# Three small tiles are allocated ahead of the large ones, which shifts the place of the large ones in a partition

## The chip, the cores and the metric

One core of one Trainium2 chip runs the whole kernel. The metric is the device time of one execution in microseconds. TensorE appears in the profile as PE (matmuls) and PEld (weight loads), VectorE as DVE, ScalarE as ACT, GpSimd as POOL, and the queue that issues most DMAs as SP.

## The reference

Two attention blocks with 32 inducing rows (m = 32) over 12480 rows of 128 channels, then two MLPs of width 2048:

```python
def mab(q, kv):
    s = scale * (q @ kv.transpose(0, 2, 1))
    s = s - s.max(-1, keepdims=True)
    a = np.exp(s)
    a /= a.sum(-1, keepdims=True) + 1e-09
    return a @ kv
h = mab(I, x)          # I: the inducing rows
y = mab(x, h)          # 12480 x 128
# first MLP
h1 = y @ w_in;  y2 = (h1 * np.cos(h1)) @ w_out
# second MLP
h2 = y2 @ w_in2; out = (h2 / (1 + np.exp(-h2))) @ w_out2
```

## The kernel before, in words

**Front.** The first part loads x, transposes it, computes the first attention with a running maximum, and folds the second attention's value product into the first MLP: `hw0` to `hw3` are the 32 rows of h times `w_in1`, four copies stacked in the 128 partitions. So the first MLP's input matmul takes the attention weights (`stk`) as its moving operand.

**Steps.** The rest is one long loop over steps, with the order written out by hand. The rows are cut into 25 blocks of up to 512 columns: 22 of 512, then 480, 448 and 288. Each block takes 8 steps (NJ = 8), and a step handles 256 of the 2048 hidden rows in two halves. In a full step TensorE does 20 matmuls, each with a 128x128 weight load of its own, in this order:

1. `mlp1_in` (line 761): 2 matmuls, weights `hw`, moving `stk`.
2. `mlp2_in` (line 896): 6 matmuls for the block that is L2 = 11 steps behind. The operands are split in a high and a low part, three products for each half: weights `wi2_0`, `wi2_1`, `wi2_0`, moving `yhi`, `yhi`, `ylo`.
3. `mlp2_out` (`down`, line 843): 6 matmuls, weights `wo2_0` and `wo2_1`, moving `hi2` and `lo2`, two steps further behind.
4. `mlp1_out` (`down` again, line 843): 6 matmuls, weights `wo1_0` and `wo1_1`, moving `hi1` and `lo1`.

Steps 3 and 4 are the same function on other tiles, so in the profile both stand at line 843 as `acc<-hi,wo` and `acc<-lo,wo` (buffer numbers are left out). They follow each other within a step, `wo2` first. In a few steps after a softmax exponential (`held_back`) `mlp2_in` comes later, and the order is 1, 3, 2, 4 or 1, 3, 4, 2.

The first 12 steps of the first MLP and the first 8 of the second use float32 weights (`wf1`, and `wf2` in `held`) with four matmuls of line 853 in the profile in place of the six of line 843. So of the steps whose block has 512 columns, 22 x 8 = 176, all have a `hw` group, 176 have a `wi2` group, 168 a `wo2` group and 164 a `wo1` group in three products.

Between the groups, ACT takes the cosine (line 796) and the SiLU (line 911) out of PSUM and makes the second MLP's high part (line 919), DVE makes the first MLP's product, high part and low part (lines 800, 807, 833), and POOL makes the second MLP's low part (line 920).

**Tiles.** The pool `persist` places its tiles one after the other in each partition, each rounded up to 32 bytes; the pools of the front (`pp`, `pw`) and of the steps (`u1`, `u2`, `blk`, `late`) lie behind it. The order in which the tiles are made thus sets their addresses.

Of the kernel before, what the change touches and what calls it, by code (L numbers as in the profile page):

```python
# [9 lines left out]
F32 = mybir.dt.float32  # L10
F32R = mybir.dt.float32r
BF16 = mybir.dt.bfloat16
I32 = mybir.dt.int32
# [9 lines left out]
def tile_induced_attention_then_two_mlps(  # L23
# [36 lines left out]
    P, G, Q = 128, 4, 32  # L60
# [6 lines left out]
    KT = 16  # L67
# [15 lines left out]
    persist = ctx.enter_context(tc.tile_pool(name="persist", bufs=1))  # L83

    half_pi = persist.tile([P, 1], F32, name="half_pi")
    quarter = persist.tile([P, 1], F32, name="quarter")
    s_w = persist.tile([P, 1], F32, name="s_w")
    hT4 = persist.tile([C, G, M], F32, name="hT4")

    held = persist.tile([P, G * W], F32, name="held")  # L90
# [3 lines left out]
    wf1 = persist.tile([P, NF, C], F32, name="wf1")  # L94
    hw = [persist.tile([P, FF // 4], F32R, name=f"hw{i}") for i in range(4)]
    wo1 = [persist.tile([P, NF, C], F32R, name=f"wo1_{i}") for i in range(2)]
    flag = persist.tile([1, 1], I32, name="flag")
    stk = persist.tile([P, 2, W], F32R, name="stk")

    sft = {  # L100
        "s2": persist.tile([P, KT, M], F32, name="s2"),
        "m2": persist.tile([P, KT, 1], F32, name="m2"),
        "sm": persist.tile([P, KT, 1], F32, name="sm"),
        "at": persist.tile([P, W], F32, name="at"),
        "hi": persist.tile([P, W], F32R, name="ahi"),
    }
# [1001 lines left out]
```

## Time and profile before

| | before |
|---|---|
| time, median of 3 runs | 967.84 us (967.08 to 967.96) |
| time of the profiled execution | 967.38 us |
| its span, first to last instruction | 965.2 us |
| PE busy | 951.8 us (99%) |
| DVE busy | 779.3 us (81%) |
| ACT busy | 691.6 us (72%) |
| POOL busy | 517.2 us (54%) |
[...]

A matmul's busy time in these views begins at its start and ends at a modelled end that reaches into the next matmul, so neighbouring ones overlap: how fast the engine advances is read from the distance between starts. A share of PE near 100% says that it has no visible gap, not that it runs at its peak.

### The profile page before, as it was taken

Reading aid. Unit: us, or ns where it says so; the run is one execution under the profiler, and the core shown is the slowest. Engines: PE = TensorE matmul, PEld = TensorE weight load, DVE = VectorE, ACT = ScalarE, POOL = GpSimd, SP = SyncE. Lnnn points to the kernel's source line nnn. Section 1 sums busy time; section 2 is a strip of 40 time slices with the busy share of each in tenths; the row PEclk is TensorE's granted clock in tenths of the full one; section 3 lists DMA queues with packets and bytes.
Section 4 is the critical chain, followed back from the end, with each engine's and each line's share of the span. In section 5 each row is a group of like instructions: output and inputs, shape, how many; then the busy total and the mean of one; then the engine's idle time right before and its main releaser. Section 6 shows DMA issues by size and latency. Waiting matters only on the chain.

```text
span 965.2 us, 11951 instructions
## 1 busy us (share of the span) xinstructions
PE 951.8 (99%) x4480; PEld 758.0 (79%) x4481; DVE 779.3 (81%) x784; ACT 691.6 (72%) x725; POOL 517.2 (54%) x274
## 2 busy tenths in 40 slices
PE   8899999999999999999999999999999999999997
PEld 5456778888878888878888887888887888888896
DVE  4889888988887988888988887988888888878751
ACT  5687768777668776767777777777767777677774
POOL 3346545654545655554655544655455554555565
PEclk9999999999999999999999999999999999999999
DMA  9341000001010010010010010010010100100001
GB/s 356 112 138 45 6 18 11 14 20 22 2 22 12 12 22 12 12 22 12 12 22 12 12 22 12 12 22 7 17 22 1 22 14 9 21 12 5 13 11 20
DMA packets 65484, 28.19 MB, mean 29 GB/s; under 512 B 54440, under 2 KB 60040, under 8 KB 65416
## 3 DMA queue, kind: packets, MB, share of 16 engines
q1 hardware_dynamic: 64760, 27.24, 10.8%
q8 instruction: 37, 0.61, 0.3%
q14 instruction: 31, 0.25, 0.1%
q10 hardware_dynamic: 656, 0.09, 0.1%
HBM read 14.79 MB, written 6.39 MB: 22 GB/s over the span
## 4 chain that ended last, share of the span: by engine, by line
PE 95%; DMA 2%; DVE 1%; issue 0%; SPq 0%; ACT 0%; POOL 0%; ACTq 0%; POOLq 0%; DVEq 0%
PE acc L843 53%; PE h L896 28%; PE h L761 9%; PE acc L853 4%; DMA x_sb<-in_x_dram 2%; PE s L211 1%; PE pt L392 0%; PE hp L539 0%; SPq L328 0%; PE s L419 0%; DVE et L507 0%; DVE c L800 0%; DVE mx L432 0%; POOL lo L925 0%; PE misc L455 0%
## 5 line engine op out<-in xcount | busy, mean ns | idle before, releaser
L920 POOL TENSOR_TENSOR lo<-s,hi 128x1024 fp32r<-128x1024 f32 (+3 forms) x189 | 446.7, 2364 | 381.0 <-ACT hi L919 359.6
L843 PE MATMUL acc<-hi,wo 128*128 128x512 f32 (+3 forms) x1520 | 406.8, 389 | 0.0
L843 PEld LDWEIGHTS acc<-hi,wo 128*128 128x128 f32 x1520 | 282.5, 188 | 61.5 <-issue 3.7
L800 DVE TENSOR_TENSOR h<-h,c 128x1024 f32<-128x1024 f32 (+3 forms) x188 | 226.1, 1203 | 123.9 <-ACT c L796 123.7
L796 ACT ACTIVATE c<-h,half_pi 128x1024 f32<-128x1024 f32 (+3 forms) x200 | 219.2, 1096 | 146.9 <-PE h L761 146.1
L911 ACT ACTIVATE s<-h 128x1024 f32<-128x1024 f32 (+3 forms) x200 | 201.2, 1006 | 76.6 <-PE h L896 71.8
L896 PE MATMUL h<-yhi,wi 128*128 128x512 f32 (+3 forms) x800 | 244.2, 386 | 0.0
L843 PE MATMUL acc<-lo,wo 128*128 128x512 f32 (+3 forms) x760 | 232.6, 387 | 0.1
L807 DVE CAST hi<-h 128x1024 fp32r<-128x1024 f32 (+3 forms) x188 | 224.9, 1196 | 6.5
L833 DVE TENSOR_TENSOR lo<-h,hi 128x1024 fp32r<-128x1024 f32 (+3 forms) x188 | 223.9, 1191 | 5.7
L919 ACT CAST hi<-s 128x1024 fp32r<-128x1024 f32 (+3 forms) x189 | 195.3, 1033 | 6.1
L896 PEld LDWEIGHTS h<-yhi,wi 128*128 128x128 f32 x800 | 148.8, 188 | 30.7 <-issue 0.5
L843 PEld LDWEIGHTS acc<-lo,wo 128*128 128x128 f32 x760 | 141.9, 188 | 31.2 <-POOL lo L925 0.4
L896 PE MATMUL h<-ylo,wi 128*128 128x512 f32 (+3 forms) x400 | 154.3, 386 | 0.0
L761 PE MATMUL h<-stk,hw 128*128 128x512 f32 (+3 forms) x400 | 126.0, 396 | 1.4 <-ACT stk L704 0.7
L761 PEld LDWEIGHTS h<-stk,hw 128*128 128x128 f32 x400 | 74.1, 188 | 26.8 <-issue 6.5
L896 PEld LDWEIGHTS h<-ylo,wi 128*128 128x128 f32 x400 | 75.1, 188 | 15.2
L877 ACT CAST yhi<-acc 128x512 fp32r<-128x512 f32 (+3 forms) x25 | 14.4, 576 | 15.1 <-PE acc L843 15.0
L943 DVE STREAM_TRANSPOSE o<-acc 128x512 f32<-128x512 f32 (+3 forms) x25 | 17.3, 694 | 9.3 <-PE acc L843 9.3
L853 PE MATMUL acc<-c,wf 128*128 128x512 f32 x48 | 22.5, 591 | 0.0
L878 DVE TENSOR_TENSOR ylo<-acc,yhi 128x512 fp32r<-128x512 f32 (+3 forms) x25 | 16.7, 669 | 5.4 <-ACT yhi L877 5.3
L800 DVE TENSOR_TENSOR c<-h,c 128x1024 f32<-128x1024 f32 x12 | 14.6, 1216 | 2.4 <-ACT c L796 1.9
(133 smaller groups left out, 320.6 us busy)
## 6 DMA issues: line engine op xcount, KB each, us to landing
out_dram<-o SPq DMA_DIRECT2D x80, 64.0 KB, 1.9
x_sb<-in_x_dram SPq DMA_DIRECT2D x8, 512.0 KB, 9.2
raw<-in_moe_w_in_dram SPq DMA_DIRECT2D x8, 512.0 KB, 6.5
raw<-in_moe_w_out_dram SPq DMA_DIRECT2D x8, 512.0 KB, 4.5
stk<-ahi SPq DMA_DIRECT2D x40, 64.0 KB, 2.0
stk<-at SPq DMA_DIRECT2D x40, 64.0 KB, 2.0
x_sb<-in_x_dram SPq DMA_DIRECT2D x3, 256.0 KB, 3.7
x_sb<-in_x_dram SPq DMA_DIRECT2D x2, 320.0 KB
```

Of the source, the lines that this page charges most:

```text
L761: nc.tensor.matmul(ps[:, a, 0:n], lhsT=hw[f // 4][:, f % 4 * P : (f % 4 + 1) * P], rhs=stacks[b][:, 0:n], start=True, stop=True,)
L796: nc.scalar.activation(cs, h, AF.Sin, bias=half_pi, scale=1.0)
L800: nc.vector.tensor_tensor(cs if whole else h, h, cs, ALU.mult)
L807: nc.vector.tensor_copy(hi[:, :, 0:n], h)
L833: nc.vector.tensor_tensor(lo[:, :, 0:n], h, hi[:, :, 0:n].bitcast(F32), ALU.subtract)
L843: nc.tensor.matmul(acc[:, 0:n], lhsT=wt[:, 2 * j + a, :], rhs=gt[:, a, 0:n], start=(j == 0 and p == 0 and a == 0), stop=(j == NJ - 1 and p ...
L853: nc.tensor.matmul(acc[:, 0:n], lhsT=w[:, 2 * j + a, :], rhs=c[:, a, 0:n], start=(j == 0 and a == 0), stop=(j == NJ - 1 and a == 1),)
L896: nc.tensor.matmul(ps[:, a, 0:n], lhsT=wt[:, fs], rhs=yt[:, 0:n], start=(p == 0), stop=(p == 2),)
L911: nc.scalar.activation(sv, hid2.pop(u)[:, :, 0:n], AF.Silu)
L919: nc.scalar.copy(hv, sv)
L920: nc.gpsimd.tensor_tensor(lv, sv, hv.bitcast(F32), ALU.subtract)
L943: nc.vector.transpose(o.rearrange("p t d -> p (t d)")[:, 0:n], acc2.pop(b)[:, 0:n])
```

## The change

`flag` (4 bytes in one partition), `m2` and `sm` (64 bytes each) are allocated right behind `s_w`, instead of behind `wo1` and `s2`. They take 32 + 64 + 64 = 160 bytes there. Nothing else is edited.

```diff
     s_w = persist.tile([P, 1], F32, name="s_w")
+    flag = persist.tile([1, 1], I32, name="flag")
+    m2 = persist.tile([P, KT, 1], F32, name="m2")
+    sm = persist.tile([P, KT, 1], F32, name="sm")
     hT4 = persist.tile([C, G, M], F32, name="hT4")
...
     wo1 = [persist.tile([P, NF, C], F32R, name=f"wo1_{i}") for i in range(2)]
-    flag = persist.tile([1, 1], I32, name="flag")
     stk = persist.tile([P, 2, W], F32R, name="stk")
 
     sft = {
         "s2": persist.tile([P, KT, M], F32, name="s2"),
-        "m2": persist.tile([P, KT, 1], F32, name="m2"),
-        "sm": persist.tile([P, KT, 1], F32, name="sm"),
+        "m2": m2,
+        "sm": sm,
```

In the two built programs the instructions, their order on every engine, their shapes and their waits are the same one by one; only addresses differ. Start of each tile in its partition, modulo 512 bytes:

| tiles | before | after |
|---|---|---|
| `hT4`, `held`, `xT`, `wf1`, `hw0` to `hw3`, `wo1_0`, `wo1_1` | 224 | 384 |
| `stk`, `s2` | 256 | 384 |
| `at`, `ahi`, `raw`, `body`, `tail`, `sign` | 384 | 384 |
| `c`, `hi1`, `lo1`, `s`, `hi2`, `lo2`, `yhi`, `ylo`, `wi2_0`, `wi2_1`, `wo2_0`, `wo2_1`, `o` | 384 | 384 |
| the front's own tiles (`x_sb`, `win`, `xF` at 192, and others) | as they are | the same |

Weights are taken in slices of 128 float32 columns, 512 bytes, and the moving halves lie 2048 bytes apart, so each slice and each half has the place of its tile modulo 512. Of the 20 matmuls of a step, the 12 on `wi2` and `wo2` have weights and moving operand at 384 in both kernels. The 6 on `wo1` go from weights at 224 and moving operand at 384 to both at 384; the 2 on `hw` go from 224 and 256 to both at 384. All tiles from `at` on keep their addresses to the byte.

## Rows read from the trace of the kernel before

**Rows 1.** Page, part 1: busy us, share of the span, instructions.

```profile
PE 951.8 (99%) x4480; PEld 758.0 (79%) x4481; DVE 779.3 (81%) x784; ACT 691.6 (72%) x725; POOL 517.2 (54%) x274
```

**Rows 2.** Page, part 4: the chain that ended last, by line.

```profile
PE acc L843 53%; PE h L896 28%; PE h L761 9%; PE acc L853 4%; DMA x_sb<-in_x_dram 2%; PE s L211 1%; PE pt L392 0%; PE hp L539 0%; SPq L328 0%; PE s L419 0%; DVE et L507 0%; DVE c L800 0%; DVE mx L432 0%; POOL lo L925 0%; PE misc L455 0%
```

**Rows 3.** Windows, PE alone: stretch, us, busy (count), granted clock, DMA share, GB/s.

```profile
123.00:846.00 723.00, 723.00 (x3162) 1.00 0.07 15
```

**Rows 4.** Timeline, PE, one step: start us, us, engine line op xcount.

```profile
264.94 0.62 PE L761 MATMUL h<-stk,hw 128*128 128x512 f32 x2
265.39 0.63 PE L896 MATMUL h<-yhi,wi 128*128 128x512 f32 x2
...
266.09 0.61 PE L896 MATMUL h<-yhi,wi 128*128 128x512 f32 x2
...
266.77 1.07 PE L843 MATMUL acc<-hi,wo 128*128 128x512 f32 x4
...
268.13 1.10 PE L843 MATMUL acc<-hi,wo 128*128 128x512 f32 x4
...
269.53 0.62 PE L761 MATMUL h<-stk,hw 128*128 128x512 f32 x2
```

**Rows 5.** Timeline, PE, the start of a step 19 steps earlier.

```profile
177.66 0.62 PE L761 MATMUL h<-stk,hw 128*128 128x512 f32 x2
178.12 0.63 PE L896 MATMUL h<-yhi,wi 128*128 128x512 f32 x2
...
178.81 0.62 PE L896 MATMUL h<-yhi,wi 128*128 128x512 f32 x2
```

**Rows 6.** Timeline, PE, a held-back step: hw, then wo2, wi2, wo1.

```profile
307.61 0.63 PE L761 MATMUL h<-stk,hw 128*128 128x512 f32 x2
308.08 1.09 PE L843 MATMUL acc<-hi,wo 128*128 128x512 f32 x4
...
309.46 0.61 PE L896 MATMUL h<-yhi,wi 128*128 128x512 f32 x2
...
310.82 1.10 PE L843 MATMUL acc<-hi,wo 128*128 128x512 f32 x4
...
312.23 0.62 PE L761 MATMUL h<-stk,hw 128*128 128x512 f32 x2
```

**Rows 7.** Timeline, PE, late step: first MLP at 480 columns, second at 512.

```profile
865.10 1.03 PE L843 MATMUL acc<-hi,wo 128*128 128x480 f32 x4
...
866.40 0.60 PE L761 MATMUL h<-stk,hw 128*128 128x480 f32 x2
866.83 0.62 PE L896 MATMUL h<-yhi,wi 128*128 128x512 f32 x2
...
868.19 1.07 PE L843 MATMUL acc<-hi,wo 128*128 128x512 f32 x4
```

**Rows 8.** Groups by shape, PE, 266.76 to 267.9 (wo2): xcount | busy us, mean ns.

```profile
L843 PE MATMUL acc<-hi,wo 128*128 128x512 f32 x4 | 1.1, 389 | 0.0
```

**Rows 9.** The same view, 268.12 to 269.3 (wo1).

```profile
L843 PE MATMUL acc<-hi,wo 128*128 128x512 f32 x4 | 1.1, 396 | 0.0
```

**Rows 10.** Groups by shape, PE, 123 to 846.

```profile
L843 PE MATMUL acc<-hi,wo 128*128 128x512 f32 x1245 | 338.3, 393 | 0.0
L896 PE MATMUL h<-yhi,wi 128*128 128x512 f32 x624 | 193.7, 391 | 0.0
L843 PE MATMUL acc<-lo,wo 128*128 128x512 f32 x622 | 193.7, 392 | 0.0
L896 PE MATMUL h<-ylo,wi 128*128 128x512 f32 x313 | 122.4, 391 | 0.0
L761 PE MATMUL h<-stk,hw 128*128 128x512 f32 x306 | 95.0, 391 | 0.0
```

**Rows 11.** Groups by shape, whole span: the longest of DVE and of POOL.

```profile
L920 POOL TENSOR_TENSOR lo<-s,hi 128x1024 fp32r<-128x1024 f32 x168 | 404.4, 2407 | 355.6 <-ACT hi L919 336.3 <-issue 12.0 <-POOL lo L920 7.3
...
L800 DVE TENSOR_TENSOR h<-h,c 128x1024 f32<-128x1024 f32 x164 | 201.9, 1231 | 104.6 <-ACT c L796 104.4
```

## The prediction

> **What bounds the kernel now.** I read the page's busy times first: PE is busy 99% of the span, DVE, the next, 81% [rows 1]. The chain of work that ended last confirms it: the matmuls of lines 843, 896 and 761 make up 53%, 28% and 9% of it, and the load of x, which is the front's share, 2% [rows 2]. [...] So a shorter time can only come from matmuls that follow each other faster, and everything that makes them follow faster counts in full as long as no other engine is late.
>
> The timeline gives the distance between starts. One full step runs from the `stk,hw` row at 264.94 to the next at 269.53, 4.59 us [rows 4]; over 19 steps it is (264.94 - 177.66) / 19 = 4.594 us [rows 4, 5]. That is 20 matmuls, 0.2297 us each. Within the step the four groups are, as differences of starts [rows 4]: `hw` 0.45 us (2 matmuls), `wi2` 1.38 (6), `wo2` 1.36 (6), `wo1` 1.40 (6). The last two are the same function on the same shapes with the same clock, and differ by 0.04 us. The groups by shape show it at nanosecond resolution: a matmul on `hi` is counted as 389 ns in the `wo2` group and as 396 ns in the `wo1` group [rows 8, 9]. These durations contain a modelled end, so only their difference is used: 7 ns a matmul, 6 x 7 = 42 ns a group, which agrees with the starts.
>
> **What could make `wo1` slow.** What the table of places says of the two groups is that `wo2` has weights and moving operand at the same place modulo 512 (384 and 384), `wo1` has 224 and 384. Their PSUM tiles differ too, and their place in the step. The place in the step can be tested in this trace. In the held-back step the order is `hw`, `wo2`, `wi2`, `wo1`, and the groups take 1.38, 1.36 and 1.41 us [rows 6]. So `wo1` is slow wherever it stands; and of the two groups on equal places, whichever comes directly behind `hw` takes 1.38 and the other 1.36. The extra 0.02 is thus not of `wi2` but left over from `hw`, whose operands stand at 224 and 256. In the ordinary step it lies in the first three of six: 265.39 to 266.09 is 0.70, 266.09 to 266.77 is 0.68 [rows 4]; in another step the first three take 0.69 [rows 5]. In the late steps, where the first MLP's block has 480 columns, `wi2` behind `hw` takes 866.83 to 868.19, 1.36 us, with nothing left over [rows 7]. So the operands at equal places have 1.36 us for six, 0.2267 us a matmul, as their undisturbed spacing, found in three surroundings.
>
> **The change part by part.** It adds and removes no instruction, wait or transfer. What moves is the place of `hw`, `stk`, `wo1`, and of the float32 tiles.
>
> - `wo1`: 164 groups from 1.40 to 1.36, 164 x 0.04 = 6.6 us.
> - `wi2` (or `wo2`) directly behind `hw`: 176 groups from 1.38 to 1.36, if `hw` at equal places leaves nothing over, 176 x 0.02 = 3.5 us.
> - `hw` itself: 0.45 us for two is already 2 x 0.2267 = 0.453. Nothing.
> - Blocks of 480, 448 and 288 columns: 24 steps. Between nothing and what a full step gains, 24 x 0.06 = 1.4 us. `wo1` at 480 columns takes 1.30 us, 0.217 each [rows 7], nearer to undisturbed, so I take nothing.
> - The float32 matmuls (line 853, 4% of the chain [rows 2], 39 us): their weights go from 224 to 384. No row shows them at 384. The bound is the relative effect on `wo1`, 0.04 / 1.40 = 3% either way, 1.2 us; I take nothing, since the chain shares of the groups that do show an effect are 20 times as large.
> - The scores on `hT4` (line 211, 1% of the chain [rows 2]): by the same 3%, 0.3 us at most either way. Nothing.
> - `flag`, `m2`, `sm` themselves: small operands of other engines at new addresses, off the path that PE sets. Nothing; if DVE were late, the cover would be gone, but see below.
>
> The sum is 6.6 + 3.5 = 10.1 us. As a check by another view, the groups by shape between 123 and 846: if every matmul there were counted as 389 ns, the savings would be 1245 x 4 + 624 x 2 + 622 x 3 + 313 x 2 + 306 x 2 ns = 9.3 us [rows 10]. The window holds 624 + 313 = 937 of the 176 x 6 = 1056 `wi2` matmuls, so the whole comes to about 9.3 x 1056 / 937 = 10.5.
>
> **Who could be late instead.** A step would become 20 x 0.2267 = 4.53 us. DVE does three operations of the size of line 800, 1.231 us, in a step, 3.7 us, POOL one of 2.407 us [rows 11]; both fit in 4.53, and ACT is busier than POOL but less so than DVE [rows 1]. DVE's 81% become 82%. The waits of PE that exist stand at the chunk boundaries and in the first steps, and one step shortened by 0.06 can grow a wait there by no more than that; at some ten places that is 0.6 us, and I take nothing.
>
> [...] The row shows two groups of equal work at 1.36 and 1.40 us [rows 4]. [...]
>
> **The rivals.**
> 1. *Only `wo1` recovers.* What `hw` leaves over comes from something else in `mlp1_in` than its places, such as its bank or its first-of-a-group position. For it: in both orders of the step the excess is tied to being behind `hw` [rows 4, 6], and not to a place of the matmuls that show it. Against it: behind `hw` at 480 columns it is absent [rows 7]. Time 967.4 - 6.6 = 960.8.
> 2. *No change.* `wo1` is slow by its PSUM bank or by what the engines do beside it, not by its place. Against it: 1.40 and 1.41 in two different surroundings [rows 4, 6]. Nothing in the rows separates the bank from the place, since `acc1` always has the same one. Time 967.4.
> 3. *Slower.* Equal places have two rhythms in this trace, 0.2267 us and, in the three matmuls behind `hw`, 0.69 to 0.70 for three, some 0.2317 [rows 4, 5]. Today the step passes `hw` and falls into the quick one. If the uniform layout settles in the slow one all through, a step takes 20 x 0.2317 = 4.63, 0.04 more than 4.594, and some 170 steps give +7 us, 974. It decides where the mean spacing exceeds today's 0.2297. Against it: wherever the trace shows equal places for more than six matmuls, the second half runs at the quick rhythm.
> 4. *A much faster rhythm* once nothing in the step differs, such as 0.225, which today's `hw` has (0.45 for two [rows 4]): a step of 4.50, 0.094 less, 176 steps, -16.5 us, 951. For it speaks no longer stretch of this trace.
>
> **How the numbers follow.** A change of 0.2%, 1.9 us, is about what a measurement can tell from none. The forecast, both terms recovered, has a chance of 0.70: the natural comparison of `wo1` with `wo2` stands in the trace, and only the bank is not excluded. Rival 1 gets 0.11, rival 2 gets 0.10, rival 3 gets 0.07, rival 4 gets 0.02. The profiled execution took 967.38 us, 2.18 more than its span, and lies 0.46 below the median of 967.84. 967.38 - 10.1 = 957.3 against the profile, 957.7 against the median; I say 957.4. The forecast's own range is 955 to 959.5: from 10.1 + 1.4 + 1.2 = 12.7 us less, with the narrow and the float32 blocks at their bounds, to about 8 less, with the starts' rounding against me. With rival 1 in it the range is 955 to 963, which leaves out rivals 2, 3 and 4, 0.19. Faster 0.70 + 0.11 + 0.02 = 0.83, same 0.10, slower 0.07.
>
> **What would show it.** In the profile after, the distance between `stk,hw` rows should be 4.53 us in the middle, the `wo1` group 1.36 us from its start to the next `hw`, the first three of `wi2` 0.68. The mean durations of all five kinds of matmul in the middle should be 389 ns. DVE, ACT and POOL durations should be what they were, and the main loop should begin at the same time. The prediction is wrong if `wo1` stays at 1.40 (rival 2), if `wi2` stays at 1.38 with `wo1` at 1.36 (rival 1), if all groups are even but above 0.2297 a matmul (rival 3), or if PE shows new gaps.

## The result and the profile after

957.9 us against 967.9 us, ratio 0.9896, interval 0.9878 to 0.9913: faster by about 10 us, 1.0%. The profiled execution took 957.71 us against 967.38, with a span of 955.5 us against 965.2, 9.7 us less. (Line numbers are two higher than before.)

The busy times come first, from part 1 of the page after, then the windows view of PE in the same stretch of the middle as before (columns as there):

```profile
PE 941.5 (99%) x4480; PEld 757.7 (79%) x4481; DVE 778.2 (81%) x784; ACT 691.9 (72%) x725; POOL 516.1 (54%) x274
```

```profile
123.00:846.00 723.00, 723.00 (x3203) 1.00 0.07 15
```

PE's busy time moved by -10.3 us, that of the other engines by 1.1 us at most [rows 1]. In the same 723 us, at the same granted clock of 1.00, it starts 3203 matmuls in place of 3162 [rows 3], 1.3% more. Neither "99% busy" nor "no gap" tells this: both read the same for either kernel.

The timeline after, PE: the start of a step; 19 steps later a whole step; a held-back step; and a late one with 480 columns.

```profile
172.21 0.61 PE L763 MATMUL h<-stk,hw 128*128 128x512 f32 x2
...
258.34 0.61 PE L763 MATMUL h<-stk,hw 128*128 128x512 f32 x2
258.80 0.62 PE L898 MATMUL h<-yhi,wi 128*128 128x512 f32 x2
...
259.48 0.62 PE L898 MATMUL h<-yhi,wi 128*128 128x512 f32 x2
...
260.15 1.07 PE L845 MATMUL acc<-hi,wo 128*128 128x512 f32 x4
...
261.51 1.07 PE L845 MATMUL acc<-hi,wo 128*128 128x512 f32 x4
...
262.88 0.62 PE L763 MATMUL h<-stk,hw 128*128 128x512 f32 x2
...
305.07 0.62 PE L763 MATMUL h<-stk,hw 128*128 128x512 f32 x2
305.52 1.07 PE L845 MATMUL acc<-hi,wo 128*128 128x512 f32 x4
...
306.88 0.61 PE L898 MATMUL h<-yhi,wi 128*128 128x512 f32 x2
...
308.24 1.07 PE L845 MATMUL acc<-hi,wo 128*128 128x512 f32 x4
...
309.60 0.61 PE L763 MATMUL h<-stk,hw 128*128 128x512 f32 x2
...
860.16 1.03 PE L845 MATMUL acc<-hi,wo 128*128 128x480 f32 x4
...
861.46 0.57 PE L763 MATMUL h<-stk,hw 128*128 128x448 f32 x2
```

The step is (258.34 - 172.21) / 19 = 4.533 us, where it was 4.594 [rows 4, 5]. Its groups, as differences of starts: `hw` 0.46, `wi2` 1.35, `wo2` 1.36, `wo1` 1.37; rounding makes the 0.01. All of these are 0.2267 us a matmul (4.533 / 20). The held-back step, with `wo2` directly behind `hw`, has 0.45, 1.36, 1.36 and 1.36, where it had 1.38 behind `hw` and 1.41 for `wo1` [rows 6]. The `wo1` group of 480 columns takes 1.30 us, as before [rows 7].

Starts rounded to 0.01 us are coarse for this. Spacings given below in ns are means of the differences of starts in the trace, over the full steps in the usual order between 123 and 846 us, 132 in nearly every run. By them the four groups went from 454.1, 1375.0, 1361.7 and 1402.5 ns to 453.3, 1360.0, 1360.0 and 1360.0.

The groups by shape after, PE, 123 to 846, answer to [rows 10]:

```profile
L845 PE MATMUL acc<-hi,wo 128*128 128x512 f32 x1255 | 336.1, 389 | 0.0
L898 PE MATMUL h<-yhi,wi 128*128 128x512 f32 x632 | 194.5, 389 | 0.0
L845 PE MATMUL acc<-lo,wo 128*128 128x512 f32 x626 | 192.7, 389 | 0.0
L898 PE MATMUL h<-ylo,wi 128*128 128x512 f32 x316 | 122.9, 389 | 0.0
L763 PE MATMUL h<-stk,hw 128*128 128x512 f32 x306 | 94.8, 391 | 0.0
```

Every kind on the split operands of `wi` and `wo` has come to the 389 ns that `wo2` alone had [rows 8]; `hw` stays at 391, where the prediction had 389 for all five. The float32 matmuls, whose weights went from 224 to 384 as well, are counted as long as before; the same view over the whole span, before and then after:

```profile
L853 PE MATMUL acc<-c,wf 128*128 128x512 f32 x48 | 22.5, 591 | 0.0
L855 PE MATMUL acc<-c,wf 128*128 128x512 f32 x48 | 22.5, 592 | 0.0
```

The longest operations of the other engines, in that view, are as long as before to within 5 ns [rows 11]:

```profile
L922 POOL TENSOR_TENSOR lo<-s,hi 128x1024 fp32r<-128x1024 f32 x168 | 403.5, 2402 | 347.3 <-ACT hi L921 328.6 <-issue 11.7 <-POOL lo L922 6.9
...
L802 DVE TENSOR_TENSOR h<-h,c 128x1024 f32<-128x1024 f32 x164 | 201.8, 1231 | 96.1 <-ACT c L798 95.9
```

### The profile page after: what moved, and what is told of

Its sections match the earlier page's. It is cut to its first block, busy times and chain, and to the rows that moved or that the text cites. A ratio compares the mean times of both kernels' runs of the same rounds, so it can differ in the third digit from the quotient of the medians.

```text
span 955.5 us, 11951 instructions
## 1 busy us (share of the span) xinstructions
PE 941.5 (99%) x4480; PEld 757.7 (79%) x4481; DVE 778.2 (81%) x784; ACT 691.9 (72%) x725; POOL 516.1 (54%) x274
## 4 chain that ended last, share of the span: by engine, by line
PE 96%; DMA 2%; DVE 1%; issue 0%; ACT 0%; SPq 0%; POOL 0%; ACTq 0%; POOLq 0%; DVEq 0%
PE acc L845 53%; PE h L898 28%; PE h L763 9%; PE acc L855 4%; DMA x_sb<-in_x_dram 2%; PE s L213 1%; PE pt L394 0%; PE hp L541 0%; PE s L421 0%; DVE et L509 0%; SPq L330 0%; DVE c L802 0%; DVE mx L434 0%; PE misc L457 0%; POOL lo L927 0%
## 5 line engine op out<-in xcount | busy, mean ns | idle before, releaser
L845 PE MATMUL acc<-hi,wo 128*128 128x512 f32 (+3 forms) x1520 | 401.7, 386 | 0.0
L845 PE MATMUL acc<-lo,wo 128*128 128x512 f32 (+3 forms) x760 | 230.2, 384 | 0.1
```

Source lines behind the costliest of these rows:

```text
L845: nc.tensor.matmul(acc[:, 0:n], lhsT=wt[:, 2 * j + a, :], rhs=gt[:, a, 0:n], start=(j == 0 and p == 0 and a == 0), stop=(j == NJ - 1 and p ...
```

## The experiments

Two questions were open: is it the place itself (384 is a multiple of 128, 224 an odd multiple of 32) or the relation of two places; and which matmuls have to share it. All runs do the full computation with the same matmuls in the same order.

**All tiles 32 bytes further on.** A pad behind `sm`.

```diff
     sm = persist.tile([P, KT, 1], F32, name="sm")
+    pad = persist.tile([P, 8], F32, name="pad")
```

> All tiles of the steps, weights and moving operands alike, lie 32 bytes further on than in the kernel after: all at 416 modulo 512 in place of 384. Theory 1 (the relative place of weights and moving operand decides): as the kernel after, 957.9 us, a ratio to before of 0.990, steps of 4.533 us. Theory 2 (the place itself decides: 384 is a multiple of 128, while 224 is an odd multiple of 32 as 416 is): no longer quick, near the kernel before, 967 us, the hw and wo1 groups at least at their old spacing, and perhaps slower still since wi2 and wo2 lose the place as well (20 matmuls at the 0.234 us of wo1 would make steps of 4.68 us, 980 us).

Measured: ratio to before 0.9897 (0.9881 to 0.9914), the kernel after's 0.9896. The timeline, PE, one step:

```profile
258.18 0.62 PE L764 MATMUL h<-stk,hw 128*128 128x512 f32 x2
...
262.71 0.61 PE L764 MATMUL h<-stk,hw 128*128 128x512 f32 x2
```

4.53 us. Theory 2 falls: 416, an odd multiple of 32 bytes, is as good as 384. What counts here is a relation between places.

**`wo1` alone back at 224.** Its line goes ahead of the three small tiles.

```diff
+    wo1 = [persist.tile([P, NF, C], F32R, name=f"wo1_{i}") for i in range(2)]
     flag = persist.tile([1, 1], I32, name="flag")
...
-    wo1 = [persist.tile([P, NF, C], F32R, name=f"wo1_{i}") for i in range(2)]
```

> As the kernel after, with only wo1_0 and wo1_1 back at 224; hw, stk and everything else stay at 384. If the terms of the prediction are separate: the wo1 group back at 1.40 us, hw and wi2 at 0.227 us a matmul, 164 x 0.04 = 6.6 us over the kernel after, 964.5 us. If instead the wo1 group needs the old hw before it to be slow, or hw alone makes the excess of the whole step: 958 to 961 us.

Measured: ratio 0.9976 (0.9966 to 0.9985), 0.0080 above the kernel after, 7.7 us where 6.6 was expected. Its timeline:

```profile
255.16 0.62 PE L763 MATMUL h<-stk,hw 128*128 128x512 f32 x2
255.62 0.62 PE L898 MATMUL h<-yhi,wi 128*128 128x512 f32 x2
...
256.98 1.07 PE L845 MATMUL acc<-hi,wo 128*128 128x512 f32 x4
...
258.34 1.10 PE L845 MATMUL acc<-hi,wo 128*128 128x512 f32 x4
...
259.74 0.62 PE L763 MATMUL h<-stk,hw 128*128 128x512 f32 x2
```

`wi2` and `wo2` 1.36, `wo1` 1.40, step 4.58. With `hw` in place `wo1` is slow by itself, and leaves next to nothing behind it: `hw` takes 457.6 ns in place of 453.3, `wi2` 1360.0 as in the kernel after.

**`hw` alone back at 224.** In the same way, the line of `hw` ahead of the small tiles; `stk` stays at 384.

```diff
+    hw = [persist.tile([P, FF // 4], F32R, name=f"hw{i}") for i in range(4)]
     flag = persist.tile([1, 1], I32, name="flag")
...
-    hw = [persist.tile([P, FF // 4], F32R, name=f"hw{i}") for i in range(4)]
```

> As the kernel after, with only hw0 to hw3 back at 224; stk stays at 384 (in the kernel before it was at 256), wo1 at 384. If the terms are separate: the hw group and the group behind it carry the excess of 0.02 us or somewhat more (the difference of places is now 160 bytes, as for wo1), 3.5 to 5 us over the kernel after, 961.4 to 963 us. If what hw left over came from stk at 256 and not from its weights: 958 us.

Measured: ratio 0.9965 (0.9951 to 0.9979), 0.0069 above the kernel after, 6.7 us, more than expected. Its timeline:

```profile
255.47 0.62 PE L763 MATMUL h<-stk,hw 128*128 128x512 f32 x2
255.93 0.63 PE L898 MATMUL h<-yhi,wi 128*128 128x512 f32 x2
...
257.32 1.08 PE L845 MATMUL acc<-hi,wo 128*128 128x512 f32 x4
...
258.69 1.07 PE L845 MATMUL acc<-hi,wo 128*128 128x512 f32 x4
...
260.05 0.62 PE L763 MATMUL h<-stk,hw 128*128 128x512 f32 x2
```

The two matmuls on `hw` take 0.46 us; most of the cost stands behind them, 1.39 for `wi2` and 1.37 for `wo2`, whose own places are equal. What `hw` leaves over thus does come from its place. In the kernel before, with `hw` 32 bytes from `stk`, only 1.38 and 1.36 stood behind it [rows 4]. That the smaller distance is the reason is not shown: `stk` moved too, and 32 bytes in every matmul cost nearly as much as 160, as the table further down shows.

**One group with a place of its own.** `wi2`, `yhi` and `ylo` lie 96 bytes further on, at 480; `wo2` goes ahead of them, in a pool of its own, to stay.

```diff
+    late2 = ctx.enter_context(tc.tile_pool(name="late2", bufs=1, reuse_waits="tile"))
+    gap = ctx.enter_context(tc.tile_pool(name="gap", bufs=1))
     blk = ctx.enter_context(tc.tile_pool(name="blk", bufs=2, reuse_waits="tile"))
...
-        wo2 = [late.tile([P, NF, C], F32R, name=f"wo2_{i}") for i in range(2)]
+        wo2 = [late2.tile([P, NF, C], F32R, name=f"wo2_{i}") for i in range(2)]
+        gap.tile([P, 24], F32, name="pad")
```

> As the kernel after, with wi2, yhi and ylo (and o) all 96 bytes further on, at 480, so that this group has weights and moving operand at one place, but another than the three other groups. If only the difference within a group counts: 957.9 us, all spacings 0.2267 us, except perhaps the two matmuls at the borders of the group. If the whole step has to share one place: spacings over 0.23 us in the six matmuls of wi2 or in those behind them, 176 x 0.02 to 0.04 = 3.5 to 7 us more, 961 to 965 us.

Measured: ratio 1.0025 (1.0015 to 1.0034), 969.7 us: slower than the kernel before, 0.0129 or 12.5 us above the kernel after, and above the 961 to 965 us of the second expectation. Its timeline:

```profile
256.34 0.62 PE L766 MATMUL h<-stk,hw 128*128 128x512 f32 x2
256.79 0.63 PE L901 MATMUL h<-yhi,wi 128*128 128x512 f32 x2
...
258.18 1.09 PE L848 MATMUL acc<-hi,wo 128*128 128x512 f32 x4
...
259.57 1.08 PE L848 MATMUL acc<-hi,wo 128*128 128x512 f32 x4
...
260.94 0.62 PE L766 MATMUL h<-stk,hw 128*128 128x512 f32 x2
```

Each of the 20 matmuls has its weights and its moving operand at equal places, and still the groups take 0.45, 1.39, 1.39 and 1.37, the step 4.60. So the pair that has to agree here is not the two operands of one matmul alone. At the two borders of the group, the weights of a matmul lie elsewhere than the moving operand of the one before it, and both borders are followed by slow matmuls, 1.39 us for six. Whether it is this crossed pair that disturbs, or the jump of the weights' or of the moving operand's own place at the border, these runs do not separate.

**Constant differences.** That left a third theory: only a change of places costs, and a constant difference is as good as none. Here all weights lie at 480 and all moving operands d bytes further on, with `gap` of d bytes and `gap2` of 512 - d. To make room, `hT4` and `s_w` go to the front's pool and one copy `hT` of 128 bytes stays, which costs one small DVE copy in the front.

```diff
-    s_w = persist.tile([P, 1], F32, name="s_w")
...
-    hT4 = persist.tile([C, G, M], F32, name="hT4")
+    hT = persist.tile([C, M], F32, name="hT")
...
+    gap = persist.tile([P, 40], F32, name="gap")
     stk = persist.tile([P, 2, W], F32R, name="stk")
...
+        late.tile([P, 88], F32, name="gap2")
         wi2 = [late.tile([C, FF], F32R, name=f"wi2_{i}") for i in range(2)]
```

> All weights of the steps (hw, wi2, wo2, wo1) at 480 and all their moving operands (stk, yhi, ylo, hi1, lo1, hi2, lo2) at 128: the difference is 160 bytes for every one of the 20 matmuls, what it was for wo1 alone in the kernel before, and nothing changes from one matmul to the next. One small copy is added in the front (a single copy of hT). Theory 1 (the weights' place has to equal the moving operand's): every matmul at the 0.2337 us of wo1 or worse, steps of 4.67 us or more, 980 us. Theory 3 (what costs is the change of places from one matmul to the next, after which the rhythm has to be found again; any constant difference is as good as none): steps of 4.533 us, 958 us.

> The same with weights at 480 and moving operands at 224, a difference of 256 bytes, half of 512, in all 20 matmuls. Theory 1: as far from equal as can be, at or above the spacing of wo1, 980 us or more. Theory 3: 958 us, steps of 4.533 us.

> The same with weights at 480 and moving operands at 32, a difference of 64 bytes in all 20 matmuls. Theory 1: slower than the kernel after, by less or as much as at 160 bytes, 965 to 980 us. Theory 3: 958 us, steps of 4.533 us.

> The same with weights at 480 and moving operands at 320, 352 bytes on or 160 bytes behind modulo 512. Theory 1: as the uniform 160, 980 us, if the sign doesn't matter. Theory 3: 958 us, steps of 4.533 us. Neither expects less than 957 us; a spacing below 0.2267 us would say that equal places are not the best ones.

The first four left open with which modulus the difference counts; three more differences followed:

> As the other uniform kernels, weights at 480, moving operands at 96, a difference of 128 bytes in all 20 matmuls. If the difference counts modulo 128 (what 0, 256, 64, 160 and 352 leave open): steps of 4.533 us, 958 us. If it counts modulo 256: the farthest from equal, at or above the 4.57 to 4.69 us of the other differences, 965 to 983 us or more.

> The same with moving operands at 160, a difference of 192 bytes. Modulo 128 this is 64: steps of 4.58 us, 965 us as the uniform 64. Modulo 256 it is -64: no value foretold, 965 us only if the sign doesn't matter.

> The same with moving operands at 0 (512), a difference of 32 bytes. Modulo 128 this is what 160 is: steps of 4.69 us, 983 us. Modulo 256, or if the cost grows with the distance from equal: no more than the uniform 64, 958 to 965 us.

Measured, with the step as the distance of two `stk,hw` rows of the timeline over the number of steps between them, and the mean ns of `hi,wo` (`wo1` and `wo2`) in 123 to 846:

| d, bytes | ratio to before | step, us | mean ns |
|---|---|---|---|
| 0 (kernel after) | 0.9896 (0.9878 to 0.9913) | (258.34 - 172.21) / 19 = 4.533 | 389 |
| 32 | 1.0138 (1.0119 to 1.0156) | (258.71 - 160.71) / 21 = 4.667 | 395 |
| 64 | 0.9979 (0.9968 to 0.9991) | (255.86 - 159.73) / 21 = 4.578 | 392 |
| 128 | 1.0105 (1.0087 to 1.0123) | (260.17 - 162.17) / 21 = 4.667 | 395 |
| 160 | 1.0159 (1.0142 to 1.0176) | (259.84 - 161.44) / 21 = 4.686 | 396 |
| 192 | 1.0125 (1.0107 to 1.0143) | (256.48 - 163.14) / 20 = 4.667 | 395 |
| 256 | 0.9910 (0.9894 to 0.9927) | (254.88 - 159.68) / 21 = 4.533 | 389 |
| 352 | 1.0132 (1.0115 to 1.0149) | (258.58 - 160.58) / 21 = 4.667 | 395 |

At 128 bytes the step of the table is that of one stretch only. The start of that stretch, its end, and two rows 19 steps apart further on:

```profile
162.17 0.63 PE L767 MATMUL h<-stk,hw 128*128 128x512 f32 x2
...
260.17 0.63 PE L767 MATMUL h<-stk,hw 128*128 128x512 f32 x2
...
317.28 0.63 PE L767 MATMUL h<-stk,hw 128*128 128x512 f32 x2
...
405.58 0.64 PE L767 MATMUL h<-stk,hw 128*128 128x512 f32 x2
```

The later steps take (405.58 - 317.28) / 19 = 4.647 us. Of the 133 full steps in the usual order, 31 take 4.667 us and 102 take 4.64 to 4.65, 4.652 in the mean over all, which fits the ratio, lower than that of 192 bytes. So one and the same layout has two lasting rhythms, and the places alone do not say which one a stretch takes. At each of the seven other differences all such steps agree to within 0.008 us.

The groups by shape at d = 160, and then at d = 256, PE, 123 to 846:

```profile
L849 PE MATMUL acc<-hi,wo 128*128 128x512 f32 x1224 | 336.4, 396 | 0.0
```

```profile
L849 PE MATMUL acc<-hi,wo 128*128 128x512 f32 x1252 | 335.2, 389 | 0.0
```

Theory 3 falls: with a constant 160 bytes all four groups are as slow as `wo1` was, 396 ns [rows 9]. Theory 1 holds for 160 and 352, and 64 lies at the lower end of its range with 965.2 us, but it falls at 256, which is as good as 0. A difference that has to be zero modulo 256 fits all eight; but no other two differences that are equal modulo 256 were tried, so the period itself is not shown. Modulo 128 is excluded by 128 itself, and by 192, which does not do what 64 does. The cost does not grow with the distance either: 32 is worse than 64, and its 980.6 us meet neither of its two expectations. None is quicker than the kernel after.

**One group 128 bytes on.** The fourth experiment once more in the roomier layout, d = 0, with a pad of 128 bytes ahead of `blk` in place of 96.

```diff
-        gap.tile([P, 24], F32, name="pad")
+        gap.tile([P, 32], F32, name="pad")
```

> All tiles of the steps at 480 and equal, only wi2, yhi and ylo (and o) 128 bytes further on: the group has one place of its own again, as in the run with 480 against 384, but now 128 bytes from the others in place of 96. If differences count modulo 128, also at the borders of the group: steps of 4.533 us, 958 us. If modulo 256 or 512: disturbed like the one at 96 bytes, 965 to 970 us.

Measured: ratio 0.9948 (0.9930 to 0.9966), between the two expectations, 0.0052 or 5.0 us above the kernel after. Its timeline:

```profile
256.01 0.62 PE L768 MATMUL h<-stk,hw 128*128 128x512 f32 x2
256.47 0.62 PE L903 MATMUL h<-yhi,wi 128*128 128x512 f32 x2
...
257.84 1.07 PE L850 MATMUL acc<-hi,wo 128*128 128x512 f32 x4
...
259.20 1.07 PE L850 MATMUL acc<-hi,wo 128*128 128x512 f32 x4
...
260.56 0.62 PE L768 MATMUL h<-stk,hw 128*128 128x512 f32 x2
```

0.46, 1.37, 1.36 and 1.36: the borders cost 0.02 us a step in all, where 96 bytes cost 0.07. A break of 128 bytes is not free either, but each border widens only two spacings, to 232.5 and 230.8 ns; the others are 226.7.

This run also speaks to a rival that the uniform layouts leave open. ACT, DVE and POOL write the tiles that TensorE reads as moving operands, so there the weights' distance to what these engines touch changed along with their distance to the moving operand. Here `wi2` lies 128 bytes from `c`, `s`, `hi1`, `lo1`, `hi2` and `lo2`, but not from its own moving operand, and its inner matmuls keep the 226.7 ns.

## Why the prediction was right, point by point

**What bounds it: right.** The time came out of the spacing of the matmuls alone: 9.7 us of span, 10.3 us of PE's busy time, no new wait of PE in the steps, and the longest DVE and POOL operations as long as before to within 5 ns.

**The undisturbed spacing: right.** 0.2267 us, read from `wo2`, became that of all four groups.

**The terms.** The forecast of 957.4 us met 957.9. Its sum of 10.1 us met 9.7 of span, in part by luck, since its two parts were off in opposite directions. By the mean spacings `wo1` gained 42.5 ns a group, 164 x 0.0425 = 7.0 us where the sum had 6.6; putting `wo1` back alone cost 7.7. The 3.5 for what `hw` leaves behind was too large: `wi2` gained 15.0 ns, 176 x 0.015 = 2.6 us, and `wo2` 1.7 ns, 168 x 0.0017 = 0.3. I had taken 1.38 - 1.36 = 0.02 us from rows rounded to 0.01. The cross-check of 10.5 counted 2 ns for each `hw` matmul, 0.6 of its 9.3 us, which `hw` did not gain; without it, it gives 9.8. `hw`, the float32 matmuls and the narrow blocks at nothing were right (391 ns before and after for `hw`, 591 and 592 for the float32 matmuls, 1.30 us for 480 columns).

**The rivals.** Only `wo1` recovering is excluded by the 1.35 of `wi2` behind `hw`, and the run with `hw` alone at 224 shows that it is `hw`'s place that the next groups pay for. No change is excluded, with the PSUM bank: `acc1` kept its bank, and its group went from 1402.5 to 1360.0 ns. The rival on the slower side was nearer than its 0.07 suggests: uniform layouts that do settle in a slow rhythm exist, at constant differences of 32, 128, 160, 192 and 352 bytes (4.65 to 4.69 us), and at 128 bytes one layout has two rhythms, as that rival supposed of equal places. That equal places are not among them was known from `wo2`, 1.36 us for six [rows 4]. The quicker rhythm of 0.225 appeared nowhere as a lasting one: the 0.45 us of `hw` in the kernel before was one spacing of 230.0 and one of 224.1 ns.

**What the relative place costs.** The same matmuls at the same granted clock, 1.00 between 123 and 846 us in both runs, follow each other every 226.7 ns with all operands at equal places and every 234.3 ns with all of them 160 bytes apart (4.533 / 20 and 4.686 / 20). By what means the places act is not shown.

What stays open is the mechanism. The runs show that the difference matters, that matmuls whose own operands agree were slowed behind one pair that differs (`wi2` 1.39 us in place of 1.36 behind `hw` at 224), and that of the eight differences tried 0 and 256 bytes alone gave steps of 4.533 us. They don't show why a step takes 4.578 us at 64 bytes and 4.667 at 32, what chooses between the two rhythms at 128, or whether 256 bytes would be free at the border of a group as well, which wasn't tried.

## What to carry to other kernels

When TensorE has no gap and one group of matmuls still starts at a larger distance than another of the same shape, compare the addresses of the weights and the moving operands: here places that were equal, or 256 bytes apart throughout, gave 0.2267 us a matmul of 512 columns, and others up to 0.234. The float32 matmuls (591 and 592 ns) and the `wo1` group of 480 columns (1.30 us) did not change. What had to agree here is the whole stream, not each group for itself, since one group with a place of its own, 96 bytes off, made the kernel slower than the kernel before (ratio 1.0025, 969.7 us). Take such small differences over many steps, or from a view with nanoseconds, since single starts rounded to 0.01 us mis-size them.

## What the runs showed of the hardware that was not expected

- A difference of 256 bytes between all weights and all moving operands was as good as none (4.533 us a step), while at 128 a step takes 4.65 to 4.67; the differences didn't order by size (32: 4.667, 64: 4.578).
- A slow spacing outlasted its cause: with only `hw` 160 bytes off, the twelve matmuls behind it, all on equal places, take 1.39 + 1.37 us in place of 2.72, 0.04 more, all of it in the first eight.
- The same places held two rhythms: with 128 bytes between all operands, steps of 4.667 us in one stretch and of 4.647 in another.
